# A hand-written start for the first two tiles, and a new place for the gate preparation and for tiles 6 and 7

## The chip, the cores and the metric

The kernel runs on one core of a Trainium2 chip. The metric is the device time of one execution in microseconds, the median of three runs. TensorE is PE in the rows below (its weight loads PEld), VectorE is DVE, ScalarE is ACT, GpSimd is POOL, and SP issues most of the transfers.

## What is computed

```
attention, per batch and head:   state (48 x 48) starts at 0; for t in 0..767:
    y[t]  = r[t] @ (state + (u*k[t]) v[t]^T)
    state = w[t][:, None] * state + k[t] v[t]^T
x = y as 3072 tokens x 384
x = ELU(x @ w_in) @ w_out                     384 -> 2048 -> 384
logits = x @ w_gate + modality_bias[modality_id];  e = argmax, gate = softmax(logits)[e]
out = gate * relu(x @ w1[e]) @ w2[e]          8 experts, 384 -> 1024 -> 384
```

The inputs w_in and w_out come as 64-bit floats, and the kernel turns them into 32-bit floats itself.

## The kernel before

**Attention in tiles.** The recurrence is cut into 24 tiles of 128 time steps (6 steps in time by 4 batches; tiles 0 to 3 are the first in time). `A1` makes the cumulative products of w with one scan (L348, DVE) over the decay w that ACT has pre-scaled (L347), their reciprocals (Ln and Exp on ACT, L351 and L352, and a Newton step of two instructions on DVE, L353 and L354), and for tiles from 6 on a two-part split of v, `vb` (L337 and L338). `A2` multiplies r and k by them (POOL, L399), forms r*k for the diagonal (`rkp`, POOL, L384; the diagonal's matmul is L410) and transposes k (L416). `A3` makes the scores (L439) and masks them (L448, DVE). `A4` multiplies by v (L482), adds the diagonal (y, L499, DVE), splits the result in two halves (ACT L506, POOL L508), transposes it (L375) into `xT`, and `upd` carries the state (L518). Two tiles make a group; there are 12 groups. The decay's products live in two buffers, RK0 for even tiles and RK1 for odd ones.

**The first layer in units.** For each group the hidden size is cut into 8 units of 256. `ffn_in` (L536, 18 matmuls) fills a bank of PSUM, ELU is made of two ACT passes (L543, L544), one DVE combine (`e`, L545), and the split into the ring (ACT L547, POOL L334). Two banks "f" take turns, so that unit n+2 can't start on PE until the combine of unit n has read its bank. `ffn_out` (L560, 12 matmuls) multiplies by w_out and collects over the 8 units. I count units through the groups: unit 8 is the first of group 1. The e of unit n is the n-th L545 on DVE, counted from 0.

**Decoding.** w_in and w_out come in 8 chunks each. A chunk is decoded from its 64-bit form by six DVE instructions in two halves (L282, L283, L284 for each half, through PSUM bank pso2), scaled and rounded by two ACT passes (L296, L299), and its low part is made by POOL (L300). Their order is wi0, wi1, wi2, wo0, wi3, wo1, ... wi7, wo5, wo6, wo7: 16 chunks, 96 DVE instructions. `ffn_in` of unit k needs chunk wi k, `ffn_out` needs wo k.

**What sets the order.** The program is written as a list of steps (`ORD` for tiles 0 to 3, then times planned by `run_steps`), and a list scheduler reorders the instructions of each engine when the kernel is built, so that the order on the chip is not the written one. `setup2` prepares the gate: it loads w_gate, the modality of each token and the bias, each by a transfer that ACT issues, splits w_gate (ACT L231, DVE L232), casts the modality (DVE L236), transposes it on PE (L238), and makes `bsel` (DVE L241 to L249). It is written at the first unit of group 1, but the scheduler had moved its first parts to the start of the kernel.

Of the kernel before, what the change touches and what calls it, by code (L numbers as in the profile page):

```python
# [10 lines left out]
F32 = mybir.dt.float32  # L11
# [38 lines left out]
def _pow2(n):  # L50
    return float(2.0 ** n)
# [78 lines left out]
def body(ctx, tc, r, k, v, w, u, rk, ul, w_in, w_out, mod, w_gate, bias, w1, w2, cst, out, dbg=None):  # L130
# [85 lines left out]
    def setup():  # L216
        nc.scalar.preload_act_table_set("natural_log_exp_and_others")
        nc.scalar.dma_start(cs, cst)
        nc.scalar.dma_start(u2, u)
        nc.vector.tensor_copy(id16, cc("ident"))  # L220
        nc.gpsimd.memset(nel, -_pow2(PH))
        nc.vector.memset(bnd, 0.0)
        nc.vector.memset(bnd[:, 0::HW], _pow2(SR))
        nc.gpsimd.memset(run_, 0.0)
# [38 lines left out]
    def prep(n, dst, key, sc, mode):  # L263
        mode = int(mode)
        if key not in staged:
            prep_load(key)
        st = staged[key]
        k0 = SEQ.index(key)
        prep_(n, dst, st, sc, mode)
        for q in range(k0 + 1, min(k0 + 1 + PLD, len(SEQ))):  # L270
            if SEQ[q] not in staged:
                prep_load(SEQ[q])

    def prep_(n, dst, st, sc, mode):
        if wide:
            t = s0.tile([128, 768], I32, tag="sti", name="sti")
            sv = st.rearrange("p (x t) -> p x t", t=2)
            hi, lo = sv[:, :, 1], sv[:, :, 0]
            for o in (0, 384):
                pt = psum(PDT[0]).bitcast(I32)[:, 0:384]  # L280
                h_, l_ = hi[:, o:o + 384], lo[:, o:o + 384]
                nc.vector.tensor_scalar(pt, h_, 3, 0x3FFFFFFF, op0=ALU.logical_shift_left, op1=ALU.bitwise_and)  # L282
                nc.vector.scalar_tensor_tensor(pt, h_, -0x40000000, pt, op0=ALU.bitwise_and, op1=ALU.bitwise_or)  # L283
                nc.vector.scalar_tensor_tensor(  # L284
                    t[:, o:o + 384], l_, 29, pt, op0=ALU.logical_shift_right, op1=ALU.bitwise_or
                )
            t = t.bitcast(F32)
        else:
            t = st
        fv = t.rearrange("p (a c) -> p a c", a=n)  # L290
# [49 lines left out]
    def A1(i):  # L340
# [37 lines left out]
    def A2(i):  # L378
# [149 lines left out]
    def ffn_in(g, u_):  # L528
# [21 lines left out]
    MK = [None]  # L550
    po_ = {}
# [375 lines left out]
    def moe_block(j, nt=2, hook=None, done=0, ahead=0, conv=False, load=False, x=False):  # L927
# [127 lines left out]
    )  # L1055
    n_ = 0
    for o in ORD:
        if o == "P":
            pre((0, n_))
            n_ += 1  # L1060
        else:
            at_step(int(o[0]), int(o[1:]))
    mp = mb = None
    NG = len(GR)
    LU = (NG - 1) * NU
    for n in range(NG * NU + LAG):
        if n == NU + LAG:
            early.close()
            LD[0] = early.enter_context(tc.tile_pool(name="ld", bufs=2))
            ubc[0] = LD[0].tile([128, DM], F32, tag="ubc", name="ubc", bufs=1)  # L1070
            nc.scalar.dma_start(ubc[0], ul.unsqueeze(0).broadcast_to([128, DM]))
            nc.scalar.activation(ubc[0], ubc[0], AF.Copy, scale=_pow2(SX))
        g, u_ = divmod(n, NU)
        now = start[g] + u_ * U_ * (SLOW if g == 0 else 1.0) if g < NG else 1e9
# [151 lines left out]
```

## Time and profile before

| | us |
|---|---|
| median of 3 runs (763.88 to 766.48) | 764.56 |
| the profiled execution's own time | 761.11 |
| its span, first to last instruction | 759.3 |
| busy: PE, DVE, ACT, POOL | 712.4, 525.6, 490.2, 407.7 |

The profiled execution is 1.81 us longer than its span, and it lies 3.45 us under the median of the timed runs. A row of the timeline gives the start in us from the span's start, the length, the engine, line and operation, what is written and read, how many instructions were merged, and in brackets how long the engine stood idle before it and what ended that.

### The profile page before, as it was taken

How to read it: one execution, taken by the hardware profiler on the slowest of the kernel's cores; microseconds unless marked ns; L12 is line 12 of the kernel's file. 1: busy time of each engine (PE TensorE's matmuls, PEld its weight loads, DVE VectorE, ACT ScalarE, POOL GpSimd, SP SyncE). 2: the span in 40 equal slices, each digit the busy share in tenths (PEclk: the TensorE clock that was granted, in tenths of full speed). 3: DMA queues.
4: the chain of work that ended last, by engine and by line, in shares of the span. 5: the costliest groups of instructions: out<-in, count | busy, mean ns of one | idle time of the engine just before them, and what ended most of it. 6: DMA issues, size and time to landing. Idle time of an engine off the chain costs nothing. (4 is left out here: it accounts for less than half of the span.)

```text
span 759.3 us, 17649 instructions
## 1 busy us (share of the span) xinstructions
PE 712.4 (94%) x6769; PEld 537.3 (71%) x6769; DVE 525.6 (69%) x1080; ACT 490.2 (65%) x951; POOL 407.7 (54%) x414
## 2 busy tenths in 40 slices
PE   3889998999999999999999999998997989999984
PEld 3768786777777776776777777776675667777763
DVE  6999884666747675668556745786686769767751
ACT  2567675567666676666666765477644769768752
POOL 5879789778687777677767660021034423331211
PEclk9999899999999999999999999999999999999998
DMA  9765524354323422443331101189239999999820
GB/s 290 249 208 187 164 58 120 112 107 112 93 82 85 135 65 80 99 122 99 80 78 54 33 13 33 53 292 311 85 126 214 348 300 378 302 266 267 251 85 13
DMA packets 89059, 114.77 MB, mean 151 GB/s; under 512 B 60709, under 2 KB 67018, under 8 KB 88964
## 3 DMA queue, kind: packets, MB, share of 16 engines
q1 hardware_dynamic: 84512, 102.75, 46.7%
q0 software_dynamic: 3456, 10.24, 4.9%
q8 instruction: 57, 0.93, 0.5%
q10 hardware_dynamic: 996, 0.53, 0.3%
q14 instruction: 38, 0.31, 0.1%
HBM read 90.29 MB, written 9.84 MB: 132 GB/s over the span
## 5 line engine op out<-in xcount | busy, mean ns | idle before, releaser
L560 PE MATMUL pso<-wo,ring 128*128 128x384 f16 x1152 | 214.1, 329 | 3.8 <-DVE X L569 2.5
L536 PE MATMUL psf<-xT,wi 128*128 128x256 f16 x1728 | 209.1, 275 | 2.8 <-DVE e L545 1.7
L536 PEld LDWEIGHTS <-wi 128*128 128x128 f16 x1728 | 166.3, 99 | 29.3 <-issue 3.4
L560 PEld LDWEIGHTS <-ring 128*128 128x128 f16 x1152 | 110.0, 98 | 67.9 <-issue 5.6
L334 POOL TENSOR_TENSOR ring<-e,ring 128x512 f16<-128x512 f32 x80 | 92.3, 1157 | 65.6 <-ACT ring L547 61.9
L545 DVE SCALAR_TENSOR_TENSOR e<-e,psf 128x512 f32<-128x512 f32 x96 | 65.6, 684 | 83.8 <-ACT e L544 81.3
L893 PE MATMUL pso<-W,gg 128*128 128x384 f16 x624 | 112.9, 328 | 3.2 <-DVE gg L334 3.2
L873 PEld LDWEIGHTS <-W 128*128 128x128 f16 x1008 | 93.6, 99 | 24.8 <-DMA XM<-G 3.5
L547 ACT ACTIVATE ring<-e 128x512 f16<-128x512 f32 x96 | 60.1, 626 | 56.6 <-DVE e L545 55.5
L893 PEld LDWEIGHTS <-gg 128*128 128x128 f16 x624 | 60.2, 98 | 39.7 <-DVE gg L334 5.5
L901 POOL DMA_INDIRECT out_dram<-ob,idxb x20 | 24.9, 1247 | 96.1 <-DVE ob L900 39.8
L543 ACT ACTIVATE e<-psf 128x512 f32<-128x512 f32 x96 | 56.4, 589 | 27.4 <-PE psf L536 23.5
L544 ACT ACTIVATE e<-e,nel 128x512 f32<-128x512 f32 x96 | 69.0, 719 | 2.5
L865 DVE SCALAR_TENSOR_TENSOR W<-wi,W 128x768 f16<-128x768 f32 x56 | 52.0, 953 | 20.6 <-ACT W L864 19.4
L865 DVE SCALAR_TENSOR_TENSOR W<-SG,W 128x768 f16<-128x768 f32 x56 | 52.5, 953 | 14.9 <-ACT W L864 14.8
L873 PE MATMUL psf<-XM,W 128*128 128x256 f16 (+1 forms) x540 | 60.4, 262 | 0.8 <-ACT mt L879 0.8
L334 DVE TENSOR_TENSOR gg<-mt,gg 128x256 f16<-128x256 f32 (+1 forms) x112 | 43.5, 402 | 22.5 <-ACT gg L880 21.9
L864 ACT ACTIVATE W<-SG 128x768 f16<-128x768 f32 x56 | 45.9, 836 | 15.5 <-DMA SG<-in_w_dram 13.7
L864 ACT ACTIVATE W<-wi 128x768 f16<-128x768 f32 x56 | 45.3, 836 | 15.3 <-DMA wi<-in_w_dram 10.9
L879 ACT ACTIVATE mt<-psf 128x256 f32<-128x256 f32 (+1 forms) x84 | 29.6, 360 | 30.8 <-PE psf L873 24.6
L348 DVE TENSOR_TENSOR_SCAN RK<-lw,bnd 112x520 f32<-112x520 f32 x24 | 39.0, 1626 | 7.4 <-ACT lw L347 4.3
L880 ACT ACTIVATE gg<-mt 128x256 f16<-128x256 f32 (+1 forms) x112 | 42.6, 397 | 1.6
(266 smaller groups left out, 1156.3 us busy)
## 6 DMA issues: line engine op xcount, KB each, us to landing
SG<-in_w_dram SPq DMA_DIRECT2D x28, 768.0 KB, 7.2
wi<-in_w_dram SPq DMA_DIRECT2D x28, 768.0 KB, 6.1
stg<-in_w_in_dram SPq DMA_DIRECT2D x8, 768.0 KB, 5.1
stg<-in_w_out_dram SPq DMA_DIRECT2D x8, 768.0 KB, 4.5
ld<-in_rk_dram SPq DMA_DIRECT2D x16, 384.0 KB, 3.3
lw<-in_w_dram SPq DMA_DIRECT2D x24, 227.5 KB, 3.0
lr<-in_r_dram SPq DMA_DIRECT2D x24, 224.0 KB, 3.3
lk<-in_k_dram SPq DMA_DIRECT2D x24, 224.0 KB, 3.0
```

The source lines that it names most:

```text
L334: (nc.gpsimd if pool else nc.vector).tensor_tensor(lo, f, hi, op=ALU.subtract)
L536: mm = nc.tensor.matmul(ph[:, 256 * z_:256 * z_ + 256], lhsT=wi[:, u_, a, kk, 128 * z_:128 * z_ + 128], rhs=xg[:, b_ * KD + kk, :], start= ...
L543: nc.scalar.activation(e, ph, AF.Exp, scale=_pow2(-PH))
L544: nc.scalar.activation(e, e, AF.Identity, scale=_pow2(PH), bias=nel)
L545: nc.vector.scalar_tensor_tensor(e, e, 0.0, ph, op0=ALU.min, op1=ALU.max)
L547: nc.scalar.activation(hl[:, 0], e, AF.Copy)
L560: nc.tensor.matmul(po_[g][i][:, 0:DM], lhsT=hl[:, a, z_, 128 * i:128 * i + 128], rhs=wo[:, u_, b_, z_, :], start=(u_ + z_ + n == 0), stop= ...
L864: nc.scalar.activation(o_[:, 0], i_, AF.Copy, scale=_pow2(sc))
L865: nc.vector.scalar_tensor_tensor(o_[:, 1], i_, _pow2(sc), o_[:, 0], op0=ALU.mult, op1=ALU.subtract)
L873: nc.tensor.matmul(ph[:, 0:n_], lhsT=w_[:, a, kk, 128 * m:128 * m + 128], rhs=xm[:, b_ * KD + kk, 0:n_], start=(n == 0), stop=(n == 3 * KD ...
L880: nc.scalar.activation(h2[:, 0, m, 0:n_], t_, AF.Copy)
L893: MK[0] = nc.tensor.matmul(po[:, 0:DM], lhsT=h2[:, a, m, 128 * t:128 * t + 128], rhs=w_[:, b_, m, :], start=(m == 0 and a + b_ == 0), stop ...
```

## The change

A new function `lead` writes out the work of tiles 0 and 1 and the decoding of chunks wi0 and wi1 as a fixed list; a chain of order-only edges (`in_order`) keeps each engine, SP excepted, in that order. `upd` of both tiles and the second transpose of k come behind it, as do the steps of tiles 2 and 3 and the ACT and DVE work of chunk wi2 in part (`behind`, `issue_after`). In the list r*k and the low half of x are made by DVE, where POOL had made them. Tiles 2 and 3 take their scratch from the "a" banks of PSUM and no longer from the "f" banks. Tiles 6 and 7 are put behind `LASTD`, the last decoding that had been written so far. `setup2` is put behind the last ELU instructions written before it on DVE and ACT (`LASTV`, `LASTA`), and all decoding that is left is written at the start of unit 8.

```diff
-    nc.vector.tensor_copy(id16, cc("ident"))
+        with tc.issue_after(HEAD[nc.scalar.engine]) if k0 == 2 else ExitStack():
+            prep_(n, dst, st, sc, mode)
...
+        LASTD[0] = nc.vector.scalar_tensor_tensor(t[:, o:o + 384], l_, 29, pt, op0=ALU.logical_shift_right, op1=ALU.bitwise_or).ins
...
-        y0 = psum("f" if i < EAR else "a")[0:PT].rearrange("p (r t) -> p r t", t=HF)
+        y0 = psum("a")[0:PT].rearrange("p (r t) -> p r t", t=HF)
...
-            pk = psum("f" if i < EAR else "a")
+            pk = psum("a")
...
-        nc.vector.scalar_tensor_tensor(e, e, 0.0, ph, op0=ALU.min, op1=ALU.max)
+        LASTV[0] = nc.vector.scalar_tensor_tensor(e, e, 0.0, ph, op0=ALU.min, op1=ALU.max).ins
...
-        nc.scalar.activation(hl[:, 0], e, AF.Copy)
+        LASTA[0] = nc.scalar.activation(hl[:, 0], e, AF.Copy).ins
...
+    def behind(on=True):
+        es = ExitStack()
+        for i in HEAD.values() if on else ():
+            es.enter_context(tc.issue_after(i))
+        return es
...
+        def rkprod(i):
+            rkp[i] = p2.tile([PT, QH, C], F32, tag="rkp", name="rkp")
+            nc.vector.tensor_tensor(rkp[i], ST[i]["r"], ST[i]["k"], op=ALU.mult)
...
+        def xlo(i):
+            nc.vector.tensor_tensor(x[i][:, 1, :], yf[i], x[i][:, 0, :], op=ALU.subtract)
...
+        with in_order():
+            scan(0)
+            lnexp(0)
+            zcopy(0)
+            nc.vector.tensor_copy(id16, cc("ident"))
+            prod(0, "r", 1)
+            prod(0, "k", 0)
+            rkprod(0)
+            newton(0)
+            prod(0, "k", 1)
+            prod(0, "r", 0)
+            scan(1)
+            lnexp(1)
+            zcopy(1)
+            prod(1, "r", 1)
+            prod(1, "k", 0)
+            rkprod(1)
+            diag(0)
+            newton(1)
+            prod(1, "k", 1)
+            prod(1, "r", 0)
+            scores(0)
+            diag(1)
+            masked(0, 0)
+            dvp(0)
+            dvp(1)
+            masked(0, 1)
+            scores(1)
+            dec(0, 0)
+            masked(1, 0)
+            dec(0, 1)
+            masked(1, 1)
+            av(0)
+            cvt(0)
+            av(1)
+            dec(1, 0)
+            ysum(0)
+            xhi(0)
+            dec(1, 1)
+            xlo(0)
+            cvt(1)
+            xt(0)
+            kt(0)
+            ysum(1)
+            xhi(1)
+            xlo(1)
+            xt(1)
+        with behind():
+            kt(1)
+            for i in range(2):
+                upd(i, 0, T.pop(i))
...
-        step(kind, i)
+        with behind(i < 4), tc.issue_after(LASTD[0]) if i in (6, 7) else ExitStack():
+            step(kind, i)
...
-    ORD = '00 01 10 20 11 30 P 21 31 P'.split()
...
+    for i in range(2):
+        load(2 + i)
+    lead()
...
+        if n == NU:
+            pre((1, NU - 1))
...
-            setup2()
+            with tc.issue_after(LASTV[0]), tc.issue_after(LASTA[0]):
+                setup2()
```

Behind unit 12 the order on DVE, POOL and SP is the same in both programs, and on PE and ACT it differs by swaps of neighbours in a few places near the end. The text speaks of three places before that.

**PE, from its first instruction.** psa and psf are the banks "a" and "f", pso the output banks; gg holds the products of r and k of tiles 0 to 2, u the diagonal's weights, lv is v. Before:

```order
L410 MATMUL psf<-u_102,rkp 128x2 x4
L439 MATMUL psa<-gg 128x128 x8
L416 MATMUL psf<-cs,gg 128x112 x4
L410 MATMUL psf<-u_102,rkp 128x2 x4
L482 MATMUL psa<-lv,Ab 128x48 x8
```

Now:

```order
L1043 MATMUL pso_67<-u_102,rkp 128x2 x4
L1052 MATMUL psa<-gg 128x128 x8
L1043 MATMUL pso_68<-u_102,rkp 128x2 x4
L1052 MATMUL psa<-gg 128x128 x8
L1073 MATMUL pso_67<-lv,Ab 128x48 x8
L1073 MATMUL pso_68<-lv,ohp 128x48 x8
L1091 LDWEIGHTS x
L1091 MATMUL psf<-id_83,x 128x128
```

The scores of tile 1 (the second L1052) now stand ahead of the product with v of tile 0; before they stood behind that product, the state of tile 0 (L518) and the transposes of k (L416).

**DVE around the last decoding.** L284 is the last instruction of half a chunk, L545 (now L547) the ELU combine, here of units 8 to 10, L348 (now L350) the scan, L340 the low part of the split of v. Before:

```order
L545 SCALAR_TENSOR_TENSOR e<-e,psf 128x512
L284 SCALAR_TENSOR_TENSOR sti<-stg,pso_69 128x384
L282 TENSOR_SCALAR pso_69<-stg 128x384
L283 SCALAR_TENSOR_TENSOR pso_69<-stg,pso_69 128x384
L284 SCALAR_TENSOR_TENSOR sti<-stg,pso_69 128x384
L282 TENSOR_SCALAR pso_69<-stg 128x384
L283 SCALAR_TENSOR_TENSOR pso_69<-stg,pso_69 128x384
L284 SCALAR_TENSOR_TENSOR sti<-stg,pso_69 128x384
L545 SCALAR_TENSOR_TENSOR e<-e,psf 128x512
L499 SCALAR_TENSOR_TENSOR y<-psa,dv 128x384
L545 SCALAR_TENSOR_TENSOR e<-e,psf 128x512
```

Now:

```order
L547 SCALAR_TENSOR_TENSOR e<-e,psf 128x512
L283 SCALAR_TENSOR_TENSOR pso_69<-stg,pso_69 128x384
L284 SCALAR_TENSOR_TENSOR sti<-stg,pso_69 128x384
L231 SCALAR_TENSOR_TENSOR wg<-ohp,wg 128x3x8
L235 CAST X_107<-X_107 24x128
L282 TENSOR_SCALAR pso_69<-stg 128x384
L283 SCALAR_TENSOR_TENSOR pso_69<-stg,pso_69 128x384
L284 SCALAR_TENSOR_TENSOR sti<-stg,pso_69 128x384
L350 SCALAR_TENSOR_TENSOR RK_103<-lw,bnd 112x520
L340 SCALAR_TENSOR_TENSOR vb<-lv,vb 128x384
L350 SCALAR_TENSOR_TENSOR RK_104<-lw,bnd 112x520
L340 SCALAR_TENSOR_TENSOR vb<-lv,vb 128x384
```

The first row of either piece is the combine of unit 8. The gate's split and cast (L231, L235) stand between the two halves of the last chunk, and the scans and splits of tiles 6 and 7 stand ahead of the combine of unit 9, which is the row that follows.

**ACT and POOL beside it.** On ACT now, from the ring's copy of unit 7 (L549) on:

```order
L549 ACTIVATE ring<-e 128x512
L229 DMA ohp<-in_w_gate_dram 128x3x8
L301 ACTIVATE wo<-sti 128x768
L233 DMA X_107<-in_mod_dram 24x256
L243 DMA ohp<-in_bias_dram 128x16
L230 ACTIVATE wg<-ohp 128x3x8
```

And on POOL now, up to the low part of the last chunk:

```order
L336 TENSOR_TENSOR ring<-e,ring 128x512
L401 TENSOR_TENSOR lk<-RK_103,lk 112x4x64
L401 TENSOR_TENSOR lr<-RK_103,lr 112x4x64
L401 TENSOR_TENSOR lk<-RK_104,lk 112x4x64
L401 TENSOR_TENSOR lr<-RK_104,lr 112x4x64
L302 TENSOR_TENSOR wo<-sti,wo 128x768
```

Before, the transfer of w_gate was ACT's third and came right behind its first pre-scaling of w; now it stands behind unit 7. On POOL four products of tiles 6 and 7 stand ahead of the last chunk's low part, where a ring's low part stood.

## Rows read from the trace of the kernel before

**Rows 1.** Stages (--windows): us, then busy us (count) per engine, granted clock, DMA share, GB/s.

```profile
40.00:110.00 70.00, 67.91 (x539) 54.97 (x538) 65.85 (x114) 48.87 (x87) 57.04 (x52) 0.93 0.50 155
110.00:127.00 17.00, 15.00 (x129) 10.31 (x129) 8.72 (x15) 9.17 (x21) 14.67 (x16) 1.00 0.44 120
127.00:400.00 273.00, 269.46 (x3045) 202.04 (x3043) 176.98 (x348) 182.44 (x347) 202.48 (x221) 1.00 0.37 95
```

**Rows 2.** Timeline of PE from its first matmul to unit 1.

```profile
11.45 1.84 PE L410 MATMUL psf<-u,rkp 112*128 112x2 f32 x8 [11.45 <-DVE RK L354]
13.22 3.10 PE L439 MATMUL psa<-gg 48*128 48x128 f32 x16
...
18.64 3.63 PE L482 MATMUL psa<-lv,Ab 128*128 128x48 f32 x16
...
39.97 6.30 PE L536 MATMUL psf<-xT,wi 128*128 128x256 f16 x36 [1.11 <-ACT xT L376]
```

**Rows 3.** Timeline of DVE: first scan, end of wi2, tile 1's y, unit 9's e.

```profile
4.80 1.24 DVE L348 TENSOR_TENSOR_SCAN RK<-lw,bnd 112x520 f32<-112x520 f32 x1 [3.45 <-ACT lw L347]
...
30.14 0.54 DVE L284 SCALAR_TENSOR_TENSOR sti<-stg,pso 128x384 int32<-128x384 int32 x1
...
35.92 0.56 DVE L499 SCALAR_TENSOR_TENSOR y<-psa,dv 128x384 f32<-128x384 f32 x1
...
108.97 0.68 DVE L545 SCALAR_TENSOR_TENSOR e<-e,psf 128x512 f32<-128x512 f32 x1
```

**Rows 4.** DVE by line (--lines) from 0 to 127 us: busy, mean ns, idle before.

```profile
L348 DVE TENSOR_TENSOR_SCAN RK<-lw,bnd 112x520 f32<-112x520 f32 x10 | 17.3, 1732 | 5.3 <-ACT lw L347 4.3 <-ACT pso L362 1.0
...
L448 DVE SCALAR_TENSOR_TENSOR Ab<-psa,cs 128x512 f32<-128x512 f32 x10 | 6.8, 683 | 2.6 <-PE psa L439 2.6
L338 DVE SCALAR_TENSOR_TENSOR vb<-lv,vb 128x384 f16<-128x384 f32 x2 | 3.9, 1965 | 1.0 <-ACT vb L337 1.0
L353 DVE SCALAR_TENSOR_TENSOR RK<-RK,psa 112x512 f32<-112x512 f32 x5 | 3.4, 681 | 1.7 <-ACT psa L352 1.7
...
L242 DVE TENSOR_SCALAR ohp<-ohp 128x24 f32<-128x24 f32 x1 | 1.5, 1548 | 0.0
L236 DVE CAST X<-X 24x128 f32<-24x128 int32 x1 | 1.2, 1244 | 0.0
```

**Rows 5.** Timeline of DVE and POOL: a scan and a split of v beside POOL.

```profile
22.76 3.03 DVE L348 TENSOR_TENSOR_SCAN RK<-lw,bnd 112x520 f32<-112x520 f32 x1
...
82.11 2.87 DVE L338 SCALAR_TENSOR_TENSOR vb<-lv,vb 128x384 f16<-128x384 f32 x1 [0.59 <-ACT vb L337]
82.49 1.28 POOL L384 TENSOR_TENSOR rkp<-lr,lk 112x512 f32<-112x512 f32 x1
```

**Rows 6.** Timeline of ACT: transfer of w_gate and its first use.

```profile
4.38 0.41 ACTq L230 DMA_DIRECT2D ohp<-in_w_gate_dram  x1
...
7.99 0.22 ACT L231 ACTIVATE wg<-ohp 128x24 f16<-128x24 f32 x1 [0.42 <-DMA ohp<-in_w_gate_dram]
```

**Rows 7.** Timeline of PE: unit 11's first and unit 12's last piece, waits, what follows.

```profile
111.09 0.60 PE L536 MATMUL psf<-xT,wi 128*128 128x256 f16 x4
...
125.07 0.31 PE L583 MATMUL psa<-wg,xT 128*128 128x16 f16 x6 [1.59 <-DMA xT<-X]
...
126.54 1.14 PE L560 MATMUL pso<-wo,ring 128*128 128x384 f16 x6
```

**Rows 8.** Timeline of PE: a row behind a short idle time.

```profile
77.88 1.38 PE L439 MATMUL psa<-Tr,Tk 48*128 48x128 f32 x8 [1.01 <-ACT US L524]
```

**Rows 9.** Window of the 8 us after it, columns as in the first group.

```profile
78.00:86.00 8.00, 8.00 (x41) 6.13 (x42) 6.40 (x8) 2.56 (x6) 6.91 (x7) 0.57 0.19 70
```

**Rows 10.** Timeline of PE: prices of 12, 12 and 8 matmuls in this stage.

```profile
61.60 0.99 PE L482 MATMUL psa<-gg,Ab 128*128 128x48 f32 x8
...
66.00 1.17 PE L439 MATMUL psa<-Tr,Tk 48*128 48x128 f32 x12
...
135.26 2.11 PE L560 MATMUL pso<-wo,ring 128*128 128x384 f16 x12
```

More of the change, by code (lines that the diff above doesn't have):

```diff
@@ L1 @@
-from contextlib import ExitStack
+from contextlib import ExitStack, contextmanager
 import numpy as np
@@ L254, in body @@
     PDT = ["o2"]
+    LASTD = [None]
     def prep_load(key):
@@ L268, in prep @@
         k0 = SEQ.index(key)
-        prep_(n, dst, st, sc, mode)
+        with tc.issue_after(HEAD[nc.scalar.engine]) if k0 == 2 else ExitStack():
+            prep_(n, dst, st, sc, mode)
         for q in range(k0 + 1, min(k0 + 1 + PLD, len(SEQ))):
@@ L272, in prep, with decode, parts @@
                 prep_load(SEQ[q])
-    def prep_(n, dst, st, sc, mode):
[L275 to L290, printed above, removed]
+    def decode(t, st, o):
+        if not wide:
+            nc.vector.tensor_copy(t.bitcast(F32)[:, o:o + 384], st[:, o:o + 384])
+            return
+        sv = st.rearrange("p (x t) -> p x t", t=2)
+        pt = psum(PDT[0]).bitcast(I32)[:, 0:384]
+        h_, l_ = sv[:, o:o + 384, 1], sv[:, o:o + 384, 0]
+        nc.vector.tensor_scalar(pt, h_, 3, 0x3FFFFFFF, op0=ALU.logical_shift_left, op1=ALU.bitwise_and)
+        nc.vector.scalar_tensor_tensor(pt, h_, -0x40000000, pt, op0=ALU.bitwise_and, op1=ALU.bitwise_or)
+        LASTD[0] = nc.vector.scalar_tensor_tensor(t[:, o:o + 384], l_, 29, pt, op0=ALU.logical_shift_right, op1=ALU.bitwise_or).ins
+    def prep_(n, dst, st, sc, mode):
+        t = s0.tile([128, 768], I32, tag="sti", name="sti")
+        for o in (0, 384):
+            decode(t, st, o)
+        parts(dst, t.bitcast(F32).rearrange("p (a c) -> p a c", a=n), sc, mode)
+    def parts(dst, fv, sc, mode):
         if mode == 0:
@@ L544, in ffn_in @@
         nc.scalar.activation(e, e, AF.Identity, scale=_pow2(PH), bias=nel)
-        nc.vector.scalar_tensor_tensor(e, e, 0.0, ph, op0=ALU.min, op1=ALU.max)
+        LASTV[0] = nc.vector.scalar_tensor_tensor(e, e, 0.0, ph, op0=ALU.min, op1=ALU.max).ins
         hl = ring[:, (g * NU + u_) % RING].rearrange("p a m t -> p a (m t)")
-        nc.scalar.activation(hl[:, 0], e, AF.Copy)
+        LASTA[0] = nc.scalar.activation(hl[:, 0], e, AF.Copy).ins
         lowp(hl[:, 1], e, hl[:, 0], g < len(GR) - 2)
-    MK = [None]
+    MK, LASTV, LASTA = [None], [None], [None]
     po_ = {}
@@ L972, in moe_block, with in_order @@
             moe_o(j, t, NF2 - 3, NF2)
+    HEAD = {}
+    def behind(on=True):
[3 more added lines that the diff above has]
+        return es
+    @contextmanager
+    def in_order():
+        seen = nc.cur_bb.bb.instructions
+        n0 = len(seen)
+        yield
+        last = {}
+        for i in seen[n0:]:
+            p = last.get(i.engine)
+            if p is not None:
+                tc.add_manual_dep(
+                    i, p.name, mybir.DependencyInfo(mybir.DependencyClass.NoSync, mybir.DependencyReason.DATA), reason="in_order"
+                )
+            last[i.engine] = i
+        HEAD.update({e_: i for e_, i in last.items() if e_ != nc.sync.engine})
@@ L1055, in body @@
     )
[L1056 to L1062, printed above, removed]
+    for i in range(2):
+        load(2 + i)
+    lead()
     mp = mb = None
```

90 lines of the change are left out of this document (added).

## The prediction

> **What bounds the kernel now.** I read the windows by stage first [rows 1]. From 127 to 400 us PE is busy 269.5 of 273 us, so whatever the start loses or wins against that point goes on to the end one for one: behind unit 12 the instruction order is the same in both programs. From 40 to 110 us it is otherwise. DVE is busy 65.9 of 70 us, mostly with the 96 decoding instructions, and PE's 67.9 busy us hold less work than they seem to, since the granted clock averages 0.93 and many matmuls wait on operands inside their own length. From 110 to 127 us DVE is busy 8.7 of 17 us and PE 15.0. So the time is set in two steps: DVE must reach the end of the decoding, and then PE runs off what is left. The place where the first hands over to the second is unit 11: its first matmul needs the bank that unit 9's combine reads, and that combine starts on DVE at 108.97 us [rows 3]; unit 11 starts on PE at 111.09 and unit 12 ends at 126.5, where unit 13 and the next rows of L560 take over [rows 7]. I therefore cost the change as the shift of unit 12's end.
>
> **The lead.** On PE the list leaves a chain of tile 0's scores, tile 1's diagonal and scores, and two products with v: 3.10 + 1.84 + 3.10 + 3.63 + 3.63 = 15.3 us at this stage's pace [rows 2]. The chain starts when tile 0's products are there. The scan ends at 6.0 [rows 3], Ln, Exp, the move of r*k to DVE and the Newton step (two instructions of 0.68 [rows 4]) follow, then two products on POOL, which I put at 10.8 us together; so the chain ends at 26.1. From tile 1's y to the first matmul of unit 0 it took 39.97 - 35.92 = 4.05 us before [rows 2, 3]; the transpose of k, now in between on PE and ACT, makes it some 5.4. Unit 0 would start at about 31.5 us instead of 39.97, 8.5 us earlier. That is the most visible effect, and it is worth nothing by itself if DVE paces what follows.
>
> **DVE up to the third chunk.** Up to the end of wi2, at 30.14 + 0.54 = 30.7 us [rows 3], the change takes the scans of tiles 2 and 3 away (1.24 and 3.03 [rows 3, 5]), the gate's cast (1.24 [rows 4]) and some 1.1 us of smaller gate instructions, 6.6 us in all. It adds one mask (0.68 [rows 4]), one y (0.56 [rows 3]), two r*k and two low halves of x. The last two kinds DVE has not done here: r*k is as large as a Newton instruction, so 0.68 each, at most POOL's 1.28 [rows 4, 5]; the low half I put at y's 0.56. Together 3.7, net -2.9. Against this DVE now waits for the cold PE chain at three masks, where it waited little before; I walk it to a start of wi2's end at 30.1, 0.6 us earlier, between 3 us earlier (no further wait) and 1.3 later.
>
> **DVE from there to unit 9's combine.** The instructions between the two points, counted in the two orders, are the same but for these: two more scans, tiles 2 and 3 (+2.5 at 1.24), one Newton pair, three masks and one y less (-1.4, -2.0, -0.6), and of the gate's work the split and cast (2.3 with the small casts) for the modality's five (2.9, of which L242 alone 1.55 [rows 4]). The sum is -2.0. Scans last 1.73 us on the mean and not 1.24 [rows 3, 4]: six of them instead of four cost 1.1 more. The two splits of v are on either side of the account, unchanged.
>
> **The new wait.** w_gate's transfer is now issued behind unit 7's ring copy. From its issue to its first use it took 7.99 - 4.38 = 3.6 us [rows 6]. DVE has five instructions of decoding, a combine and two small ones, 2.7 us, between unit 7's combine and the split of w_gate, while the copy (0.6), the transfer (3.6) and ACT's own split (0.2) take 4.4; the copy also queues behind a scaling of wo6, and the modality's transfer is issued after another one. I take 2.4 us of standing still, between 0 (a faster landing) and 3.6. Behind the waiting split stand the cast, the last half chunk, tiles 6 and 7 and unit 9's combine. The scan of tile 2 waits 0.6 us for its pre-scaling, which now comes behind the lead on ACT. Before, DVE stood 2.8 us in this stretch; 1.0 of that I keep. Net +1.2.
>
> So unit 9's combine comes at 108.97 - 0.6 - 2.0 + 1.1 + 1.2 = 108.7 us, 0.3 us earlier. The 8.5 us of PE's early start have gone into waiting.
>
> **PE behind it.** PE then stands idle, since its earlier rows are done, and starts unit 11 right behind the combine, at 108.7 + 0.8 = 109.5, 1.6 us earlier than 111.09. Left to the end of unit 12 are, beside what was left before, the scores (8 records), the diagonal and the product with v (16 records) of tile 5, against 11 matmuls of L560 that are already done: +0.8 + 0.8 + 2.0 + 0.5 - 1.8 = +2.3 [rows 10], with the diagonal at half its cold length [rows 2] and the transpose of k put at 0.5. Before, 15.45 us went from 111.09 to 126.54, of which 2.0 were waits, the longest 1.59 for a transposing transfer [rows 7]; in the change that transfer is issued earlier against PE, and I drop the waits. So 13.45 + 2.3 = 15.8 us, +0.35.
>
> **The clock.** Behind 1.01 us of idle PE [rows 8] the granted clock averaged 0.57 over 8 us [rows 9]: 6.9 us at the lower of the two levels, 1.2 and not 2.4 GHz, costing up to half of that, 3.4 us. The change leaves PE idle for some 3 to 5 us ahead of unit 11, so I expect the lower level at unit 11's start; how long it stays I can't tell from here. I take 1.7, between 0 and 3.4.
>
> Sum: -1.6 + 0.35 + 1.7 = +0.45 us. Against the profiled execution's own 761.11 this is 761.6; the median of the runs lies 3.45 us above that execution, so I predict 764.56 + 0.45 = **765.0 us**, that is, no difference that shows: a measurement of this kernel tells 0.3%, 2.3 us, from nothing.
>
> What costs nothing: scratch in the "a" banks, hidden while DVE has work to decode; the transfers of tiles 2 and 3, which stand on SP in the same places as before. Tiles 6 and 7 on POOL: four products of 0.7 ahead of the last chunk's low part delay `ffn_out` of unit 7, which needs that part, but by 108.7 us PE waits for unit 9's combine anyway; without that cover they would cost 2.7 us.
>
> **Rival 1, faster: the wait isn't there and PE stays at the upper level.** If w_gate lands before DVE comes to it and the clock holds, 2.4 and 1.7 us go, and 760.9 us follows; with scans at 1.24 another 2.9, 758.0. If DVE didn't pace at all, the 8.5 us of unit 0 would all come through, 756.1. For it speaks that DVE's work up to unit 9 really is smaller; against it the order, in which the gate's split stands ahead of the last half chunk. It decides at 106 us for unit 9's combine. Chance 0.26.
>
> **Rival 2, slower: POOL and DVE shut each other out at tiles 6 and 7.** One split of v lasted 2.87 us where it was issued at 82.11 beside POOL instructions that followed without a gap, where the other of the two took 2 x 1.965 - 2.87 = 1.06 [rows 4, 5]; a scan lasted 3.03 against 1.24 [rows 3, 5]. In the change two scans and two splits stand in a row ahead of unit 9's combine, while POOL has four products and a low part to run, released by these very scans. At the long lengths they cost 2 x (3.03 - 1.73) + 2 x 2.87 - 3.9 = 4.4 us more [rows 4, 5], and with the clock low for 3.4 us the sum is +6.6, 771.1 us; half of it gives 768. For it speaks that POOL's products follow each scan directly. Against it: of the ten scans most are short. It decides from 112 us for unit 9's combine on. Chance 0.29.
>
> The Trainium skill, "SBUF — State Buffer", section "Who interferes with whom", says that a VectorE instruction with two inputs in SBUF and a GpSimd instruction that reads SBUF exclude each other, for the whole instruction of whichever came first. By that rule every scan, split, r*k and low half of x here can be blocked, and this change, which puts more of them on DVE, would come out by rival 2's sum. The trace agrees in part: the 2.87 and 3.03 us rows show it, but most scans are near 1.24.
>
> **How the numbers follow.** The forecast has 0.45. Of both signs neither rival has most of the chance. The forecast's own bounds (wait 0 to 3.6, clock 0 to 3.4, lead -2.4 to +1.9) reach from 761 to 769; rival 1 reaches down to 758 and beyond, rival 2 up to 771. I leave out a tenth on either side: 759.0 to 769.5. Faster by over 0.3% (under 762.3): 0.26; within: 0.45; slower (over 766.9): 0.29.
>
> **What would show it.** Right: unit 0 on PE at 30 to 33 us, the last L284 at 100 to 104, an idle time of 1.5 to 3.5 us on DVE ahead of the split of w_gate, ended by ACT or the transfer, PE idle 3 us or more ahead of unit 11, unit 11 at 108 to 111, unit 12's end at 125.5 to 128.5. Wrong: unit 12's end before 124 or after 129; a DVE that is idle for long before 95 us, which would mean that PE or ACT pace the decoding; or a shift at unit 12 that isn't found in the whole time.

## The result, and the profile after

The changed kernel took 770.27 us (median of 20 runs, 762.46 to 777.03) where the kernel before took 764.3 in the same comparison. The ratio is 1.006, with a 95% interval of 1.0036 to 1.0085: **slower by 0.6%**, some 4.6 us. On the 764.56 us that the prediction started from, that is 769.1, just inside the stated range; the likeliest case, no difference that shows, did not come. The ratio leaves out the runs over 1.5% above the fastest of their kernel, five of the changed kernel and one of the other; the two medians, over all runs, stand as 1.0078, which would be 770.5 us, just outside the range.

The profiled execution of the changed kernel took 771.28 us, 1.0 above its median, with a span of 769.5. Against the profiled execution before that is 10.2 us, more than the medians differ by, because that one lay 3.45 under its median. Places in the trace are read from these two executions; what something is worth is read from the ratios. Single executions scatter (758.48 to 771.22 before, 762.46 to 777.03 after), so a place in one trace is one draw.

The stages after, with the columns of [rows 1]:

```profile
40.00:110.00 70.00, 61.91 (x462) 48.57 (x462) 57.17 (x108) 46.46 (x83) 50.89 (x47) 0.88 0.49 157
110.00:127.00 17.00, 14.55 (x88) 10.98 (x87) 14.17 (x21) 9.28 (x22) 13.46 (x14) 0.83 0.40 106
127.00:400.00 273.00, 270.70 (x3025) 202.81 (x3026) 174.75 (x348) 180.25 (x343) 209.37 (x229) 0.99 0.39 97
```

From 40 to 110 us DVE is busy 57.2 us and not 65.9, and PE 61.9 and not 67.9: both now stand waiting in the stage that DVE had filled. From 110 to 127 us DVE is busy 14.2 us and not 8.7, and PE issues 88 matmuls where it issued 129. The granted clock is down in both.

PE's timeline after:

```profile
34.29 1.91 PE L538 MATMUL psf<-xT,wi 128*128 128x256 f16 x9
...
42.48 1.90 PE L441 MATMUL psa<-gg 48*128 48x128 f32 x8 [1.85 <-POOL gg L401]
...
72.53 0.71 PE L441 MATMUL psa<-Tr,Tk 48*128 48x128 f32 x4 [2.56 <-ACT kf L420]
...
113.69 1.03 PE L538 MATMUL psf<-xT,wi 128*128 128x256 f16 x8 [0.65 <-DVE e L547]
...
120.49 1.25 PE L412 MATMUL psa<-u,rkp 112*128 112x2 f32 x8 [1.80 <-DVE Ab L450]
121.77 2.13 PE L562 MATMUL pso<-wo,ring 128*128 128x384 f16 x6
...
136.09 1.14 PE L562 MATMUL pso<-wo,ring 128*128 128x384 f16 x6
```

Unit 0 starts at 34.3 us, 5.7 earlier than before [rows 2]. Unit 11 starts at 113.7, 2.6 later, and unit 12 ends at 136.1, 9.55 later [rows 7]; the span is 10.2 us longer. The row at 121.77 has 6 matmuls in 2.13 us, where the row at 136.09 has as many in 1.14: PE is at the lower level there. The chain that ended last, in two stretches, shows what stood between:

```profile
66.01 0.63 POOL Tr L401
66.64 4.78 DMA lv<-in_v_dram
...
71.86 0.63 ACT kf L420
72.53 1.28 PE psa L441 x8
...
113.04 0.60 DVE e L547
...
113.80 2.70 DVE ohp L241
116.50 0.64 DVE X L247
117.14 1.23 DVE bsel L246
```

Two links in it are new. On ACT the scaling of tile 7's v waits for a transfer, with tile 4's k behind it:

```profile
71.43 0.52 ACT L339 ACTIVATE vb<-lv 128x384 f16<-128x384 f32 x1 [3.07 <-DMA lv<-in_v_dram]
71.86 0.62 ACT L420 ACTIVATE kf<-psa,cs 128x448 f32<-128x448 f32 x1
```

The change put tile 7's split of v behind the last decoding on DVE; its ACT half, which feeds a DVE instruction at 112.5 us, was not held back, and the scheduler's new order has it at 71.4. Before, it stood behind tile 4's k, right ahead of its DVE half at 82.11 [rows 5]. ACT before:

```profile
75.74 0.61 ACT L418 ACTIVATE kf<-psa,cs 128x448 f32<-128x448 f32 x1
...
81.55 0.52 ACT L337 ACTIVATE vb<-lv 128x384 f16<-128x384 f32 x1 [1.57 <-DMA lv<-in_v_dram]
```

And on DVE the gate's four small instructions stand between the combine of unit 9 and tile 5's masks:

```profile
108.80 0.55 DVE L284 SCALAR_TENSOR_TENSOR sti<-stg,pso 128x384 int32<-128x384 int32 x1
...
112.97 0.67 DVE L547 SCALAR_TENSOR_TENSOR e<-e,psf 128x512 f32<-128x512 f32 x1
113.57 0.17 DVE L240 COPY ohp<-psa 128x24 f32<-128x24 f32 x1
...
113.77 2.73 DVE L241 TENSOR_SCALAR ohp<-ohp 128x24 f32<-128x24 f32 x1
116.42 0.73 DVE L247 TENSOR_TENSOR X<-ohp 128x192 f32<-128x192 f32 x1
117.07 1.31 DVE L246 TENSOR_TENSOR bsel<-ohp 128x192 f32<-128x192 f32 x1
...
119.17 0.67 DVE L547 SCALAR_TENSOR_TENSOR e<-e,psf 128x512 f32<-128x512 f32 x1
119.76 0.68 DVE L450 SCALAR_TENSOR_TENSOR Ab<-psa,cs 128x512 f32<-128x512 f32 x1
```

The combine of unit 10 thus comes 6.2 us behind that of unit 9; before it came 3.9 behind.

### The profile page after: what moved, and what is told of

The parts are those of the page before. It is cut to its first block, busy times and chain, and to the rows that moved or that the text cites. A ratio compares the mean times of both kernels' runs of the same rounds, so it can differ in the third digit from the quotient of the medians.

```text
span 769.5 us, 17645 instructions
## 1 busy us (share of the span) xinstructions
PE 718.6 (93%) x6769; PEld 540.9 (70%) x6769; DVE 522.7 (68%) x1084; ACT 488.0 (63%) x951; POOL 402.8 (52%) x410
## 4 chain that ended last, share of the span: by engine, by line
PE 50%; DMA 23%; DVE 12%; issue 5%; ACT 4%; POOL 3%; SPq 1%; ACTq 0%; DVEq 0%; POOLq 0%
PE psf L538 19%; PE pso L562 18%; DMA out_dram<-ob,idxb 9%; DMA SG<-in_w_dram 7%; DVE W L867 3%; DMA wi<-in_w_dram 2%; PE pso L895 2%; PE psa L444 2%; ACT W L866 2%; PE psf L875 1%; DVE RK L350 1%; DMA stg<-in_w_in_dram 1%; DMA lk<-in_k_dram 1%; PE psa L484 1%; DVE e L547 1%
## 5 line engine op out<-in xcount | busy, mean ns | idle before, releaser
L538 PE MATMUL psf<-xT,wi 128*128 128x256 f16 x1728 | 211.4, 276 | 2.9 <-DVE e L547 2.1
L547 DVE SCALAR_TENSOR_TENSOR e<-e,psf 128x512 f32<-128x512 f32 x96 | 65.6, 684 | 80.2 <-ACT e L546 76.6
L549 ACT ACTIVATE ring<-e 128x512 f16<-128x512 f32 x96 | 60.1, 626 | 59.5 <-DVE e L547 59.4
L545 ACT ACTIVATE e<-psf 128x512 f32<-128x512 f32 x96 | 56.5, 589 | 25.8 <-PE psf L538 20.6
L336 DVE TENSOR_TENSOR gg<-mt,gg 128x256 f16<-128x256 f32 (+1 forms) x112 | 43.5, 402 | 12.0 <-ACT gg L882 10.4
L401 POOL TENSOR_TENSOR lk<-RK,lk 112x256 f32<-112x256 f32 x36 | 30.2, 838 | 8.6 <-DVE RK L356 6.9
```

The costliest lines, as they stand in the source:

```text
L336: (nc.gpsimd if pool else nc.vector).tensor_tensor(lo, f, hi, op=ALU.subtract)
L538: mm = nc.tensor.matmul(ph[:, 256 * z_:256 * z_ + 256], lhsT=wi[:, u_, a, kk, 128 * z_:128 * z_ + 128], rhs=xg[:, b_ * KD + kk, :], start= ...
L545: nc.scalar.activation(e, ph, AF.Exp, scale=_pow2(-PH))
L547: LASTV[0] = nc.vector.scalar_tensor_tensor(e, e, 0.0, ph, op0=ALU.min, op1=ALU.max).ins
L549: LASTA[0] = nc.scalar.activation(hl[:, 0], e, AF.Copy).ins
```

## The experiments

Ratios are against the kernel before, run beside each set. "Decoded" counts the half chunks (L284) that DVE has finished by 60 us, of 32. The last two columns are the starts of DVE's combines of units 9 and 12 in the profiled execution.

| run | ratio, 95% interval | decoded | unit 9 | unit 12 |
|---|---|---|---|---|
| before | 1 | 16 | 109.0 | 128.2 |
| the change | 1.0060 (1.0036 to 1.0085) | 12 | 113.0 | 137.8 |
| gate_free | 1.0107 (1.0062 to 1.0152) | 12 | 114.8 | 138.7 |
| t67_free | 1.0056 (1.0019 to 1.0092) | 12 | 114.9 | 135.8 |
| both_free | 1.0122 (1.0065 to 1.0178) | 13 | 119.3 | 132.6 |
| tail_only | 0.9955 (0.9924 to 0.9986) | 18 | 107.3 | 127.4 |
| tiles_loose | 1.0082 (1.0049 to 1.0114) | 14 | 116.0 | 136.8 |
| f_banks | 1.0143 (1.0101 to 1.0185) | 14 | 110.8 | 135.4 |
| pool_back | 1.0145 (1.0097 to 1.0193) | 13 | 110.7 | 134.8 |
| tail_abank | 1.0029 (0.9999 to 1.0058) | 17 | 114.1 | 130.5 |
| warm | 1.0082 (1.0050 to 1.0115) | 12 | 111.0 | 135.9 |
| tail_warm | 0.9908 (0.9879 to 0.9938) | 18 | 110.8 | 130.9 |
| tail_t67 | 1.0051 (1.0017 to 1.0084) | 14 | 114.6 | 136.9 |
| moved | 0.9996 (0.9967 to 1.0024) | 12 | 108.8 | 131.5 |

**Is it the lead or the end?** Three runs took placements at the end out of the change, one put them alone into the kernel before.

**gate_free**, the gate preparation not held back:

```diff
-            with tc.issue_after(LASTV[0]), tc.issue_after(LASTA[0]):
-                setup2()
+            setup2()
```

> The changed kernel, but the gate preparation no longer stands behind unit 7's ring copy: the scheduler may put it where it finds room (it puts the split and cast of w_gate at the start and the small instructions near the tenth chunk). Theory E (the end of the decoding costs: the gate's small instructions, 4.8 us of DVE in front of tile 5's masks, leave PE idle and let its clock drop): unit 12 ends at 130 to 133 us instead of 136.1, the low granted clock behind 121 us goes, and the time falls to 0.999 to 1.002 of the kernel before. Theory L (the lead costs: DVE waits for PE's scores between 40 and 75 us, and whatever stands at the end only takes up what is late anyway): unit 12's end stays at 135 us or later and the time stays at 1.004 to 1.008.

**t67_free**, tiles 6 and 7 not held back:

```diff
-        with behind(i < 4), tc.issue_after(LASTD[0]) if i in (6, 7) else ExitStack():
+        with behind(i < 4):
```

> The changed kernel, but tiles 6 and 7 may start before the last decoding: their scans and value splits (4.2 us of DVE in front of unit 9's combine) go back among the fourth to seventh chunks. Theory E, as far as tiles 6 and 7 are meant: unit 9's combine comes at 109 us instead of 113.0 only if DVE has had idle time to do these scans in, as it had 10.7 us of it between 32 and 113 us; then unit 11 starts at 110 and the time falls to 1.000 to 1.003 of the kernel before. Theory L: DVE's idle time lies in waits for PE that these instructions don't fill, so unit 9's combine stays at 112 to 114 us and the time at 1.004 to 1.008.

**both_free** has both edits.

> The changed kernel with both placements at the end undone, so that the lead, the scratch banks of tile 2 on and the decoding placed at unit 8 remain. Theory E: the time is that of the kernel before or below, 0.995 to 1.001, with unit 12's end at 124 to 129 us. Theory L: 1.004 to 1.008, and unit 12's end at 133 us or later; the DVE waits for PE between 40 and 75 us (3.1 and 1.8 us the longest in the changed kernel) are still there.

**tail_only** is the kernel before with `LASTD`, `LASTV` and `LASTA`, and with these lines:

```diff
-        step(kind, i)
+        with tc.issue_after(LASTD[0]) if i in (6, 7) else ExitStack():
+            step(kind, i)
...
+        if n == NU:
+            pre((1, NU - 1))
...
-            setup2()
+            with tc.issue_after(LASTV[0]), tc.issue_after(LASTA[0]):
+                setup2()
```

> The kernel before, with only the placements at the end: the gate preparation behind unit 7's ring copy, tiles 6 and 7 behind the last decoding, the last chunk's decoding written down at unit 8. The lead and the scratch banks are those of before. Theory E: the loss is there without the lead, 1.004 to 1.009 of the kernel before, with the gate's small instructions in front of tile 5's masks and unit 12's end at 131 us or later. Theory L: 0.998 to 1.002, unit 12's end at 125 to 129 us.

Undoing the end gave nothing back (1.0107, 1.0056, 1.0122), and the end alone made the kernel before faster, 0.9955: its decoding ends at 95.3 us, where it ended at 109.0 before.

```profile
94.78 0.53 DVE L285 SCALAR_TENSOR_TENSOR sti<-stg,pso 128x384 int32<-128x384 int32 x1
```

So the 1% between tail_only and the change comes with the lead and the banks. But an edit that takes a constraint away lets the scheduler write another order from there on, so these runs price whole orders. In both_free the order of DVE sets two scans beside POOL:

```profile
51.82 3.36 DVE L350 TENSOR_TENSOR_SCAN RK<-lw,bnd 112x520 f32<-112x520 f32 x1
...
79.17 3.29 DVE L350 TENSOR_TENSOR_SCAN RK<-lw,bnd 112x520 f32<-112x520 f32 x1
```

A scan is 1.24 us long where POOL leaves a gap [rows 3]. In the change none of the scans from 36 to 110 us is over 1.3 us, so undoing a part could easily make things worse.

**What in the lead?** Three runs undid one part of it, one put one part into tail_only.

**tiles_loose** takes `behind(i < 4)` away:

```diff
-        with behind(i < 4), tc.issue_after(LASTD[0]) if i in (6, 7) else ExitStack():
+        with tc.issue_after(LASTD[0]) if i in (6, 7) else ExitStack():
```

> The changed kernel, but the steps of tiles 2 and 3 need not stand behind the lead's last instruction on each engine: the scheduler puts tile 2's and tile 3's scans between the lead's masks. The first four runs left the loss with the lead. Theory A (holding tiles 2 and 3 back is what costs: their scores come late, DVE's masks wait for them with the decoding queued behind): tile 2's products and scores come some 3 us earlier, 14 or more of the 32 half chunks are decoded by 60 us instead of 12, and the time falls to 0.995 to 1.001 of the kernel before. Theory B (the banks) and theory C (the work moved from POOL to DVE): 1.003 to 1.008, 12 or 13 half chunks by 60 us.

Tile 2's products did come earlier, and 14 half chunks were decoded, but nothing came of it (1.0082). Tile 5's scan, 1.24 us in the change, met POOL:

```profile
48.68 5.89 DVE L350 TENSOR_TENSOR_SCAN RK<-lw,bnd 112x520 f32<-112x520 f32 x1
```

**f_banks** gives tile 2 its "f" banks back, in the two lines that the change had edited (`EAR` is 3, so that tile 3 had "a" banks in the kernel before too):

```diff
-        y0 = psum("a")[0:PT].rearrange("p (r t) -> p r t", t=HF)
+        y0 = psum("f" if i < EAR else "a")[0:PT].rearrange("p (r t) -> p r t", t=HF)
...
-            pk = psum("a")
+            pk = psum("f" if i < EAR else "a")
```

> The changed kernel, but tile 2's scratch (the first value of 1/x and the bank of the diagonal and of k's transpose) is in an f bank again. Theory B (three a banks for scores, scratch and products with v of tiles 2 and 3 make these wait for one another, so that PE splits the scores around other work): 14 or more half chunks by 60 us, the wait of 3.1 us at tile 2's mask gone, 0.995 to 1.001 of the kernel before. Theories A and C: 1.003 to 1.008, and the unit rows, which also use the f banks, wait more for them.

**pool_back** gives r*k and the low half of x of the lead to POOL:

```diff
-            nc.vector.tensor_tensor(rkp[i], ST[i]["r"], ST[i]["k"], op=ALU.mult)
+            nc.gpsimd.tensor_tensor(rkp[i], ST[i]["r"], ST[i]["k"], op=ALU.mult)
...
-            nc.vector.tensor_tensor(x[i][:, 1, :], yf[i], x[i][:, 0, :], op=ALU.subtract)
+            nc.gpsimd.tensor_tensor(x[i][:, 1, :], yf[i], x[i][:, 0, :], op=ALU.subtract)
```

> The changed kernel, but r*k and the low half of x of tiles 0 and 1 are done on POOL again, four instructions off DVE (1.2, 1.1, 1.5 us and one more, some 4.5 us with the waits inside). Theory C (these four are what put DVE late): the end of the decoding comes 3 to 5 us earlier, 1.000 to 1.002. Theories A and B: 1.004 to 1.009, since DVE waits for PE behind the lead in any case and POOL's products of tile 2 come no earlier.

**tail_abank** is tail_only with `"f" if i < 2 else "a"` in the same two lines.

> The kernel before with the placements at the end (0.9955 in the first four runs), and with tile 2's scratch in an a bank as in the changed kernel, while tiles 0 and 1 stay in f banks. No lead. Theory B: the banks cost without the lead too, 1.000 to 1.005, with 15 or fewer half chunks decoded by 60 us. Theories A and C: 0.993 to 0.998, 17 or 18 half chunks by 60 us.

f_banks and pool_back were slower than the change, 1.0143 and 1.0145: neither theory B nor C got its time. That clears neither, since these runs too price whole orders: f_banks has theory B's 14 half chunks, and in its trace units 9 and 12 come 2.2 and 2.4 us earlier than in the change, in pool_back's 2.3 and 3.0, so what they lost isn't in the stretch up to unit 12; in pool_back a scan that lasted 1.50 us in the change took 3.72. tail_abank fell between: its 1.0029 is theory B's number, its 17 half chunks are that of theories A and C. What the banks and the moved work are worth by themselves stays open.

**The same order, one thing changed.** From here, tail_t67 excepted, the order of every engine was held by a table (of all that is written ahead of unit 40): the numbers of the instructions in the order that the scheduler had written, chained by order-only edges, so that an edit moves only what it names. In the traces the order of PE, DVE and ACT is then that of the kernel copied, but for what the edit names and one ACT instruction behind 740 us.

```diff
+        for e_, s_ in PIN.items():
+            p = None
+            for nm in s_.split():
+                i = by.get("I-" + nm)
...
+                for j in list(range(int(nm) - k, int(nm))) + [int(nm)]:
+                    i = by[f"I-{j}"]
+                    if p is not None:
+                        tc.add_manual_dep(i, p.name, dep, reason="pin")
+                    p = i
```

**warm** adds, ahead of tile 2's scores and in their bank, 18 multiplications of the identity:

```diff
+    WARM = {(2, 0, 0): 18}
...
+        for _ in range(n):
+            FL.append(nc.tensor.matmul(o, lhsT=id16, rhs=id16, start=True, stop=True).ins)
...
+            if (i, s_, q) in WARM:
+                warm(WARM[i, s_, q], pa[0][:, 0:128])
```

> The changed kernel with the order of every engine held to what it was, by a table, and 18 extra multiplications of the identity written by PE into tile 2's score bank just ahead of its scores (the scores overwrite them), so that PE runs through most of the 1.85 us at 40.6 to 42.5 us in which it stood idle. Theory K (the low granted clock from 42 to 57 us follows that idle time, and it is the price of the lead: PE answers DVE's masks late): that stretch stays at the upper level, tile 2's scores take 0.9 and not 1.9 us, DVE's wait of 3.1 us at 51 shrinks to 1 or less, and the time falls by 3 to 5 us, to 1.000 to 1.003 of the kernel before. Theory N (the clock falls because the stretch as a whole gives PE too little to do, so that it falls a little later anyway, or PE's rate there isn't what the end hangs on): 1.004 to 1.009, 12 or 13 half chunks decoded by 60 us as before.

The clock did what theory K says. From 42 to 56 us it was granted in full, where it had been 0.65 in the change (windows, first warm, then the change):

```profile
42.00:56.00 14.00, 11.24 (x99) 9.07 (x96) 13.20 (x17) 9.00 (x19) 13.41 (x14) 1.00 0.49 150
```

```profile
42.00:56.00 14.00, 13.52 (x68) 9.88 (x68) 8.60 (x16) 7.16 (x15) 12.44 (x13) 0.65 0.47 153
```

Tile 2's scores took 1.16 and not 1.90 us, and PE issued 99 matmuls and not 68. The time did not follow (1.0082, theory N's number). DVE and PE were 3.5 to 5 us ahead by 51 us, then DVE came with its next scan just when POOL had four instructions without a gap, and PE waited for what stood behind the scan. PE, DVE and POOL of warm:

```profile
57.57 0.76 PE L461 MATMUL psa<-Tr,Tk 48*128 48x128 f32 x2 [4.21 <-DVE y L521]
```

```profile
51.36 5.14 DVE L359 TENSOR_TENSOR_SCAN RK<-lw,bnd 112x520 f32<-112x520 f32 x1
```

```profile
50.60 1.31 POOL L395 TENSOR_TENSOR rkp<-lr,lk 112x512 f32<-112x512 f32 x1
51.87 1.65 POOL L311 TENSOR_TENSOR wi<-sti,wi 128x768 f16<-128x768 f32 x1
53.47 0.83 POOL L485 TENSOR_TENSOR dv<-lv,dg 128x384 f32<-128x384 f32 x1
54.25 1.16 POOL L345 TENSOR_TENSOR ring<-e,ring 128x512 f16<-128x512 f32 x1
```

The same scan in the change:

```profile
56.35 1.24 DVE L350 TENSOR_TENSOR_SCAN RK<-lw,bnd 112x520 f32<-112x520 f32 x1 [1.44 <-ACT pso L364]
```

That is 3.9 us of scan against 3.5 to 5 us of lead, which the clock had won. PE stood idle for 4.2 us, and the low level came back, at a place where the change has none (58 to 64 us, first warm, then the change):

```profile
58.00:64.00 6.00, 6.00 (x33) 4.79 (x33) 4.82 (x9) 2.48 (x6) 3.19 (x3) 0.50 0.44 163
58.00:64.00 6.00, 5.88 (x62) 5.29 (x61) 5.66 (x12) 5.16 (x10) 3.71 (x4) 1.00 0.51 171
```

At unit 12 warm's trace is still 1.9 us ahead of the change's (135.9 to 137.8); behind it, in the same order, that is lost, and its span is 4.4 us longer (773.9 to 769.5). So filling the first idle time did not shorten the run; what the low clock costs by itself is not shown, since one low stretch took the place of another.

**tail_warm** does the same in tail_only, with 20 such matmuls ahead of tile 1's transposes of x and 8 ahead of unit 0.

> The kernel before with the placements at the end (0.9955), every engine's order held as it was, and 20 and 8 extra multiplications of the identity ahead of tile 1's transposes of x and of unit 0's first row, in banks that these then overwrite: PE waited 2.5 and 0.9 us there, and unit 0 then took 4.0 us where unit 1 took 2.1. Theory K: unit 0 takes 2.1 to 3 us, the low clock at 49 to 53 us goes or moves, and the time falls by 1 to 3 us more, 0.991 to 0.995 of the kernel before. Theory N: no difference against the placements alone, 0.993 to 0.998.

Its ratio is the best of all, 0.9908, but its interval meets that of tail_only, and the trace shows no gain at the place: unit 0 took 2.12 and not 4.00 us, then unit 1 waited 2.96 us for a Newton step on DVE, and the combines of units 0 to 5 stand within 0.3 us of those of tail_only; those of units 9 and 12 come 3.5 us later, in an execution that was the slowest of its six. Both are faster than the two kernels of this study; which of the two is faster stays open.

**tail_t67** is tail_only with `setup2()` not held back.

> The kernel before, with only tiles 6 and 7 behind the last decoding and the last chunk's decoding written down at unit 8; the gate preparation goes where the scheduler puts it. If tiles 6 and 7 are what gains (their scans and value splits, 4 us of DVE, and their products on POOL leave the decoding's stretch): 0.994 to 0.998, the decoding ends at 95 to 98 us as in the kernel with all three placements. If the gate's place gains: 0.998 to 1.002.

Neither number came: 1.0051. The scheduler's order behind that edit has a scan of 5.87 us at 55.3 and 14 half chunks decoded by 60 us. What the end's placements are worth one by one can't be read from such runs.

**moved** holds the order of the change and moves the two links named above, five instructions in all (`-` where one stood, `+` where it stands now; names shortened, rows between left out). On ACT the scaling of tile 7's v goes to 81.0 us, near its place in the kernel before:

```diff
 ACT:  -vb(7)  kf(4)  ...  kf(5)  +vb(7)
 DVE:  e(9)  L240  -L241  -L247  -L246  -L248  e(10)  mask  mask  +L241  +L247  +L246  +L248
```

> The changed kernel with the order of every engine held by a table, and five instructions in other places. On ACT, the scaling of tile 7's v, which waited 3.07 us for its transfer at 71.4 us with tile 4's k behind it though its other half follows only at 112.5, goes some 13 us later. On DVE, the gate's four small instructions (2.73, 0.73, 1.31 and 0.35 us) go from ahead of tile 5's two masks to behind them. Theory Q (these links of the chain of waits are on the path): tile 4's scores start at 70 and not 72.5 us, so that unit 4's combine comes at 80 instead of 82.6; unit 10's combine, which stood at 119.2, comes 4 to 5 us nearer to unit 9's, PE's idle time of 1.8 us at 120.5 and the low clock behind it go, unit 12 ends 4 to 8 us earlier, and the time falls to 0.996 to 1.001 of the kernel before. Theory R (what a link gives back is waited for again at the next, as 1.85 us of idle PE were in the run with the extra multiplications): the two places move as said, but unit 12's end moves by under 2 us and the time stays at 1.004 to 1.009.

Theory Q came: 0.9996, whose interval lies below that of the change. On PE tile 4's scores now stand without a wait in front of them, the 1.80 us of idle ahead of tile 5's diagonal are gone (1.40 others come at 119.5), and unit 12 ends at 128.1 and not 136.1:

```profile
68.20 1.73 PE L450 MATMUL psa<-Tr,Tk 48*128 48x128 f32 x16
...
119.54 1.32 PE L571 MATMUL pso<-wo,ring 128*128 128x384 f16 x6 [1.40 <-DVE X L580]
...
128.08 1.14 PE L571 MATMUL pso<-wo,ring 128*128 128x384 f16 x6
```

DVE of moved:

```profile
108.81 0.67 DVE L556 SCALAR_TENSOR_TENSOR e<-e,psf 128x512 f32<-128x512 f32 x1
...
110.17 0.67 DVE L556 SCALAR_TENSOR_TENSOR e<-e,psf 128x512 f32<-128x512 f32 x1
110.77 0.68 DVE L459 SCALAR_TENSOR_TENSOR Ab<-psa,cs 128x512 f32<-128x512 f32 x1
...
113.92 0.94 DVE L250 TENSOR_SCALAR ohp<-ohp 128x24 f32<-128x24 f32 x1
```

Unit 9's combine comes 4.2 us earlier (112.97 to 108.81). Of these 0.6 are there at unit 3's combine (64.27 to 63.66), ahead of the first link; 3.6 are left for that link. Unit 10's combine is another 4.8 nearer (6.20 to 1.36), the second. Of these 9.0 us 8.0 are left at unit 12's end and 6.2 in the span (763.3 to 769.5). So these two links together cost what the change lost; each was not run alone. The table is not what won: warm has it too and is no faster than the change. The first link lies in the stretch behind the lead, the second comes with the gate's new place at the end, so that "the lead or the end" has the answer: both. Beside them 16 us at a clock of 0.68 were left as they were:

```profile
42.00:58.00 16.00, 15.92 (x96) 12.13 (x96) 10.12 (x19) 8.11 (x18) 13.57 (x13) 0.68 0.42 129
```

## Why the prediction was right, and where it was wrong

**The frame held for this pair, but not one for one.** Up to unit 12 the order decides, and unit 12's shift is there at the end: 9.55 us at unit 12, 7.9 at unit 72's combine, 10.2 in the span. In other runs it is not: against the kernel before, unit 12's combine and the span are 4.4 and 13.5 us later in both_free, 7.6 and 14.6 in warm, 10.5 and 6.4 in gate_free. What is won or lost behind unit 12 no run here says. PE's early start is worth nothing by itself: unit 0 came at 34.3 (I said 31.5, before 40.0), and the 5.7 us went into waiting. In moved, too, it gains nothing: 0.9996.

**DVE to the end of wi2** came 1.8 us later than before and not 0.6 earlier (my bound was 1.3): r*k took 1.2 and 1.1 us where I had put 0.68, and one low half of x 1.53 where I had put 0.56. (The "start of wi2's end at 30.1, 0.6 us earlier" mixes two numbers: 30.14 was the start before, 30.7 the end.)

**"1.0 of that I keep" failed.** I put DVE's waits up to unit 9's combine at 4.0 us. They came to 10.7; the largest in the view of DVE's waits from 30 to 114 us (in all, times, longest):

```profile
DVE Ab L450 <- PE psa L441: 5.1, 5, 3.1
DVE RK L355 <- ACT psa L354: 1.8, 1, 1.8
DVE RK L350 <- ACT pso L364: 1.4, 1, 1.4
DVE wg L231 <- ACT wg L230: 1.3, 1, 1.3
```

The wait that I did price, for w_gate, was 1.25 us, inside 0 to 3.6 and under my 2.4. What I missed were waits behind tiles 2 to 4: their masks for PE's scores, and the Newton step behind ACT's wait for tile 7's v. I had written that the splits of v are "on either side of the account, unchanged". On DVE two are, and they even took 1.1 us and not 3.9; but ACT's half of tile 7's came in front of tile 4's k, and moved shows that it cost some 3.6 us at unit 9's combine. So that combine came at 112.97 and not at 108.7, and the last L284 at 108.8 and not by 104. That it was no later is luck: beside the splits, the six scans took 8.2 us where I had put 10.4.

**"So 13.45 + 2.3 = 15.8 us" failed most.** From unit 11's start to unit 12's end PE took 22.4 us (113.69 to 136.09). I had struck the gate's small instructions (2.9 us) out of the stretch ahead of unit 9's combine and not put them back into the stretch behind it, where they stand ahead of tile 5's masks. There they take 5.1 us (2.73 + 0.73 + 1.31 + 0.35), PE idles 1.8 us, and the low clock follows:

```profile
120.00:130.00 10.00, 9.51 (x43) 7.46 (x44) 5.08 (x10) 5.51 (x15) 8.89 (x10) 0.56 0.58 104
```

In moved that window has 0.83. For the clock I had 1.7 us, up to 3.4, at unit 11's start; it fell behind 1.85, 2.56 and 1.80 us of idle PE at three other places. In the warm run the first of these was filled, and the low level came back behind the next idle time, so that its price alone is not shown.

**Rival 2 named the right side and the right point** (slower, from 112 us for unit 9's combine on) by the wrong place. The scans and splits of tiles 6 and 7 were short (1.24, 0.54, 1.72, 0.53 us). Beside POOL a small instruction was long instead, the gate's L241: 2.73 us for 24 elements, ending with the third of POOL's instructions that ran meanwhile,

```profile
114.83 1.63 POOL L302 TENSOR_TENSOR wo<-sti,wo 128x768 f16<-128x768 f32 x1
```

and 0.94 in moved, where only the last 0.9 us of a POOL instruction lay beside it. The two behind it were longer than in moved as well (0.73 and 1.31 against 0.35 and 0.83). The Trainium skill, "SBUF — State Buffer", section "Who interferes with whom", has the same rule for a VectorE instruction that runs in a mode with two ports, and names tensor_scalar among those that may. The trace agrees in part: L241 was long beside POOL, but through three of POOL's instructions and not one. That the exclusion is what held it is argued from these rows and not tested.

**The likeliest case was wrong, the range right, and that by luck**: 1.006 is 769.1 us, 0.4 inside the upper end. The account had put unit 12's end at +0.45 us, and the traces have it at +9.55; two of its own signs of being wrong came, unit 12's end after 129 and a DVE that is idle for long before 95 us. The range held because the ratio is worth half of what the two traces differ by. My bounds don't add up to it either: taken together they reach from 758.5 to 769.8 and not from 761 to 769, and the sum of the instructions between wi2 and unit 9 is -2.1 and not -2.0.

## What to carry to other kernels

When a step is held back on one engine, look at its half on every other engine: a constraint that names an instruction of DVE holds nothing on ACT, and the half that is free can come forward and wait for a transfer in front of work that is due. An instruction that is struck out of one stretch must be put into the one where it now stands, with what is queued behind it there. In a kernel that a scheduler orders, taking a constraint out prices a new order and not the constraint; hold the order by a table and move single instructions.

## What was not expected of the hardware

A scan of 1.24 us lasted 5.14, 5.87 and 5.89 us in three orders. In the warm run, whose POOL rows are shown above, it ended 1.1 us behind the fourth POOL instruction in a row without a gap, as if it had waited for the whole train, not for one instruction. The train need not be over: in both_free the scan of 3.36 us ended 1.1 us behind the second of POOL's instructions that ran meanwhile (52.43, 1.65 us long), and the next of POOL's took 1.77 us, where the same one took 0.83 in the change. The Trainium skill, "SBUF — State Buffer", section "Who interferes with whom", says that the other engine blocks for the whole instruction of whichever issued first. Here the scan sat through two of POOL's in both_free and four in warm. So 3.9 us of the 5.0 by which DVE was early there were lost again in one instruction.

A full clock did not shorten the run: 14 us at 1.00 and not 0.65 were followed by 6 us at 0.50 and not 1.00, and the time stayed (1.0082 and 1.0060, with intervals that overlap).
